# P times V over four heads at once, in place of two heads at a time, in a two-layer attention kernel

## The chip, the cores and the metric

The kernel runs on one core of a Trainium2 chip, with data in float32. The metric is the device time of one execution in microseconds (us), as the median of several runs. The engines are called as the profile calls them: PE is TensorE (PEld its weight loads), DVE VectorE, ACT ScalarE, POOL GpSimd, SP SyncE.

## The reference

Two attention layers, A and B, each on its own input of 2048 rows by 1024, with 32 heads of width 32. A is dilated: each row attends to 8 keys, two rows apart. B is a sliding block, and it is the layer that the change touches:

```python
def _B_ref(x, wqkv, wo):
    B, S, D = x.shape
    H = 32; Dh = D // H; W = 256
    qkv = (x @ wqkv).reshape(B, S, 3, H, Dh).transpose(2, 0, 3, 1, 4)
    q, k, v = qkv[0], qkv[1], qkv[2]
    scores = jnp.einsum("bhqd,bhkd->bhqk", q, k) * (Dh ** -0.5)
    idx = jnp.arange(S)
    mask = (idx[:, None] - idx[None, :] >= 0) & (idx[:, None] - idx[None, :] < W)
    scores = jnp.where(mask[None, None], scores, -1e9)
    p = _softmax(scores, axis=-1)
    o = jnp.einsum("bhqk,bhkd->bhqd", p, v)
    return o.transpose(0, 2, 1, 3).reshape(B, S, D) @ wo
```

The outputs of A and B are concatenated.

## The kernel before

**Units and head groups.** The work is cut into eight units: four chunks of 512 rows of layer B, then four of layer A. Within a unit, the 32 heads are taken in eight groups of four heads. For a unit the kernel computes the projections to Q and K (L579) and to V (L644), the attention of each head group, and, staggered into the next unit, the output projection (L707). These large products run as three float32r matmuls each, on a high and a low part of each operand; VectorE and ScalarE make these parts from raw loads (L213, L216, L219).

**Attention of one head group in layer B.** `attention(u, s)` has two stages. In the first, 16 score matmuls (L959), a masked maximum (L964) and an exponential with a sum (L969) give the logarithm of each row's softmax sum, which is written into extra rows of the stacked Q (L998, L1004). In the second, the scores are computed anew, transposed, keys on partitions (L1043), the exponential is written as P to `pbuf` (L1050), and the triangles at the diagonal and at the far end are cleared by POOL (L1028) or DVE (L1031). Last, `values(li)` multiplies P by V (L1109). The second stage goes in two lots, `li` 0 and 1, each with its scores, exponentials, masks and one run of L1109.

**P times V.** The 128 keys of a block are cut in two halves of 64 (`r` 0 and 1), because the band of a half reaches over fewer query columns (64 + 256 at most). A matmul takes 64 keys (64 rows of the PE array, partitions 64r to 64r+63), 32 columns of V (head `j`, columns 32j to 32j+31 of the array), and streams up to 384 query columns of P. So there are eight tiles of the array, one for each pair of half and head. The half `r` = 0 accumulates in the PSUM tile `o`, the half `r` = 1 in the PSUM tile `x`, head j in partitions 32j to 32j+31 of both; `join` adds the two (L910, L915). `pieces[li]` lists the pieces of columns as (n, r, kb, q0, c): n columns of half r of key block kb. In the first unit there are no earlier keys (`has_halo` is false) and a lot has four pieces: 320, 384, 256 and 192 columns in lot 0, 320, 320, 128 and 64 in lot 1. In units 1 to 3 a lot has six: in lot 0 o 320, x 320, o 256, x 192, x 128, o 64. Each float32 matmul of the program stands in the trace as two passes, each with its own weight load.

**What sets the order.** A planner in Python (`Clock`, and the loop at the end) writes the order of the whole program out: it keeps an estimate of each engine's time and at each step takes, from the queues of attention steps (`ones`, `twos`, `aux`) and projection steps (`gemm`), the one that is ready first. A step of L1109 is one item, with a cost that the change leaves as it is. On each engine the instructions then stand in that order, and semaphores make them wait for each other. The masks of one lot are all planned to be over before its L1109 begins (`values_ready`).

**Copies of Q and K.** SP issues the copies that stack Q and K (L540) and the halo of keys (L469, L530). `later` in `evac` holds a copy back until the head group before last is through with the buffer.

Of the kernel before, what the change touches and what calls it, by code (L numbers as in the profile page):

```python
# [240 lines left out]
def kernel(ctx, tc, xs, wqk, wv, wo, outs, units):  # L241


    nc = tc.nc
# [21 lines left out]
    def parts_of(u):  # L266
        return VPARTS if len(V_AT[u]) == 3 else VPARTS_LATER
# [40 lines left out]
    for p in plan:  # L308
# [3 lines left out]
        elif p[0] == "v":  # L312
            if slots_of(p[1]).get(NG - 1) == p[2] and p[1] + 1 < U:
                continue
            s0, n = parts_of(p[1])[p[2]]
# [10 lines left out]
        else:  # L326
            u = p[1] - 1
# [8 lines left out]
    for key, i in where.items():  # L336
        u = min(key[1] + (key[0] == "o"), U - 1)
        light[i] = PACE[u][5] if units[u][2] else PACE[u][2]
    pbuf = const.tile([P, 4, NP], F32, name="pbuf")
# [73 lines left out]
    done, waiting = {}, {}  # L413
# [4 lines left out]
    class Ring:  # L418
# [21 lines left out]
        def join(self, pool, tag, t):  # L440
            i = len(self.slots)
            self.slots = self.slots[self.i:] + self.slots[:self.i] + [(pool, tag, i)]
            self.i, self.free[i] = 0, t
# [13 lines left out]
    def qk_items(u, s):  # L457
# [3 lines left out]
        hg = u * NG + s  # L461
# [4 lines left out]
        def read_halo():  # L466
            hb = halo[(u + 1) % 2][s]
            for r, a in enumerate((0, 1, 0)):
                nc.sync.dma_start(kst[buf][r:96:3, :, :256].bitcast(F32), hb[:, a])  # L469
                ck.copy("halo_in", ck.now)  # L470

        def evac_window(t, ps, bank):
            if t == 0:
                h2["qk"] = natp.tile([P, 2 * S + 16], F32R, tag="nat", name="nat").bitcast(F32)[:, :2 * S + 8]
                nc.scalar.activation(h2["qk"][:, :S], ps, AF.Copy, scale=SCALE)
                e = ck.use("act", 0.485, ck.now + ck.SEM)
                by_head(0, S, e)
            else:
                qk = h2["qk"]
                nc.scalar.copy(qk[:, S + 8:], ps)  # L480
                e = ck.use("act", 0.485, ck.now + ck.SEM)
                if has_halo:
                    nc.scalar.copy(qk[:, S:S + 8], tails[:, s, :])
                    e = ck.use("act", 0.2, e)
                else:
                    nc.vector.memset(qk[:, S:S + 8], 0.0)
                    ck.use("dve", 0.08, ck.now)
                if u + 1 < U and units[u + 1][3]:
                    nc.scalar.copy(tails[:, s, :], ps[:, S - 8:])
                    e = ck.use("act", 0.2, e)  # L490
                by_head(S, 2 * S + 8, e)
            rg.give(bank, e)
# [18 lines left out]
        def evac(t, ps, bank):  # L511
            if not dense:
                return evac_window(t, ps, bank)
            hl = natp.tile([P, 2 * S + 16], F32R, tag="nat", name="nat")[:, :2 * S].rearrange("p (a s) -> p a s", a=2)
            sc = SCALE if t == 0 else 1.0
            nc.scalar.activation(hl[:, 0, :], ps, AF.Copy, scale=sc)
            r = ck.use("act", 0.485, ck.now + ck.SEM)

            def low():
                nc.vector.scalar_tensor_tensor(hl[:, 1, :], ps, sc, hl[:, 0, :].bitcast(F32), op0=ALU.mult,  # L520
                                               op1=ALU.subtract)
                e = ck.use("dve", 0.61, r)
                rg.give(bank, e)

                def stack():
                    e2 = place(1, e)
                    if t == 1:
                        done["stack"][u, s] = max(e2, h2["hi"]) + PACE[u][1]
                    if t == 1 and u + 1 < U and units[u + 1][3]:
                        nc.sync.dma_start(halo[u % 2][s], hl[:, :, 256:].bitcast(F32))  # L530
                        e2 = ck.copy("halo_out", e, ck.now)
                    done["nat"][2 * hg + t] = max(e2, h2["hi"])

                later(stack)

            def place(part, e):
                dst, c = (qst[buf], 0) if t == 0 else (kst[buf], 256)
                for i, a in enumerate((0, 0, 1) if t == 0 else (0, 1, 0)):
                    if a == part:
                        nc.sync.dma_start(dst[i:96:3, :, c:c + S].bitcast(F32), hl[:, a, :].bitcast(F32))  # L540
                        e2 = ck.copy("copy", e, ck.now)
                return e2

            def stack_hi():
                if t == 0 and has_halo:
                    read_halo()
                h2["hi"] = place(0, r)

            def later(f):
                if hg < 2 or hg - 2 in done["second"]:  # L550
                    f()
                else:
                    waiting.setdefault(hg - 2, []).append(f)

            later(stack_hi)
            ck.defer(r, low)

        for t in range(2):
            h = {}
# [306 lines left out]
    def seat_free(hg):  # L866

        done["scores"][hg] = ck.now

        def go():  # L870
            for f in waiting.pop(("seat", hg), []):
                f()

        ck.defer(ck.now + 0.3, go)
# [61 lines left out]
    def attention(u, s):  # L936
# [4 lines left out]
        hg = u * NG + s  # L941
        q, kk = qst[buf], kst[buf]
        vp, vc = vparts[parts_of(u)][s]
        v = vbufs[parts_of(u)][vp]
        h = {"left": 16, "rows": None}
# [132 lines left out]
        pieces = []  # L1078
        for lot in lots:
            p = []  # L1080
            for kb, c, w in [x for segs, heads in lot for x in segs if heads[0] == 0]:
                q0 = max(0, kb * P)
# [5 lines left out]
            while rows_of[0] or rows_of[1]:  # L1088
                r = 0 if rows_of[0] and (not rows_of[1] or t[0] <= t[1]) else 1
# [11 lines left out]
        def values(li):  # L1101
            if not li:
                h["o"], h["begun"] = [ro.take()[0], rx.take()[0]], set()
            for j0 in (0, 2):
                for n, r, kb, q0, c in pieces[li][0]:
                    slot = (4 * u + kb) % 6
                    part = slice(64 * r, 64 * r + 64)
                    for j in (j0, j0 + 1):
                        nc.tensor.matmul(h["o"][r][32 * j:32 * j + 32, q0:q0 + n],  # L1109
                                         v[part, slot, vc + 32 * j:vc + 32 * j + 32], pbuf[part, j, c:c + n],  # L1110
                                         start=(j, r) not in h["begun"], stop=True, skip_group_check=True)
                        h["begun"].add((j, r))

            def after():
                pfree[0] = ck.now
                h["pv", li] = ck.now
                if hg == last_dense and li:
                    seat_free(hg)
                if li:
                    join(u, s, h)  # L1120

            return after

        for li, lot in enumerate(lots):
            for ci, (segs, heads) in enumerate(lot):
                two.append(Item(lambda li=li, ci=ci: second_ready(li, ci), lambda li=li, ci=ci: second(li, ci),
                                len(heads) * sum(x[2] / 2400 + 0.016 for x in segs)))
            two.append(Item(lambda li=li: values_ready(li), lambda li=li: values(li),
                            C3 + PACE[u][4] + pieces[li][1] / 592))
# [43 lines left out]
    n = TAIL  # L1173
# [92 lines left out]
```

## Time and profile before

| | |
|---|---|
| median of 3 runs | 1834.28 us (1830.59 to 1834.33) |
| the profiled execution, its own time | 1833.12 us |
| its span, first to last instruction | 1831.4 us |
| PE busy | 1809.4 us (99%) |
| DVE, ACT, POOL busy | 1245.9 us (68%), 1034.4 us (56%), 370.2 us (20%) |
| L1109, o and x, busy summed over both | 109.7 us and 109.0 us, 1408 passes each |
| mean granted TensorE clock | 0.999 |

The page of the profile gives busy time for each engine and for each group of instructions of one line. Matmuls overlap, so busy times of PE's groups add up to more than their share of the span; the time between the start of one stretch of matmuls and the start of the next instruction says more. The timeline view lists instructions by start, with those of one line and tile that follow each other merged into one row with a count.

### The profile page before, as it was taken

The page shows a single profiled execution, that of the slowest core. Times are in us where ns is not written, and L with a number is a line of the kernel's source. Part 1 is how long each engine was busy: PE and PEld are TensorE (multiplying, and loading weights), DVE is VectorE, ACT ScalarE, POOL GpSimd, SP SyncE. Part 2 cuts the span into 40 slices and gives each one's busy share as a digit, 9 for nine tenths or more (in the row PEclk, how much of TensorE's full clock was granted, in tenths as well). Part 3 has the DMA queues.
Part 4 walks back from the last instruction along what each step waited for, and adds up shares of the span by engine and source line. Part 5 has one row for each costly group of instructions (what it writes and reads, how often), then busy time and mean ns, then how long its engine had stood idle before and what let it go on. Part 6 is the DMA issues. An engine that isn't in the chain of part 4 may idle for free.

```text
span 1831.4 us, 37311 instructions
## 1 busy us (share of the span) xinstructions
PE 1809.4 (99%) x14186; PEld 1504.5 (82%) x14186; DVE 1245.9 (68%) x2632; ACT 1034.4 (56%) x2552; POOL 370.2 (20%) x835
## 2 busy tenths in 40 slices
PE   8999999999999999999999999999999999999999
PEld 6788788888887888788888878888888888878887
DVE  6578866667766567666666486886777567866674
ACT  5567676666666665766666544552445255644452
POOL 3212222233321222322222400011001100110000
PEclk9999999999999999999999999999999999999999
DMA  7355654546545546455455253345335443544332
GB/s 231 101 152 146 175 159 139 156 144 165 156 139 156 150 127 188 121 153 148 129 145 170 66 160 118 128 131 156 128 109 162 133 137 105 162 129 137 118 111 81
DMA packets 109140, 257.38 MB, mean 141 GB/s; under 512 B 14497, under 2 KB 29857, under 8 KB 108961
## 3 DMA queue, kind: packets, MB, share of 16 engines
q0 software_dynamic: 41760, 152.06, 27.0%
q1 hardware_dynamic: 56832, 83.00, 16.9%
q10 hardware_dynamic: 10368, 19.93, 3.0%
q8 instruction: 112, 1.84, 0.4%
q14 instruction: 68, 0.55, 0.1%
HBM read 164.63 MB, written 23.07 MB: 102 GB/s over the span
## 4 chain that ended last, share of the span: by engine, by line
PE 87%; DMA 4%; DVE 3%; issue 3%; ACT 2%; SPq 0%; POOL 0%; ACTq 0%; POOLq 0%; DVEq 0%
PE g L579 29%; PE g L707 15%; PE g L644 13%; PE x L579 6%; PE s L1043 6%; PE s L959 5%; PE o L1109 4%; PE x L707 3%; PE x L644 3%; PE o L843 2%; PE x L1109 1%; PE s L777 1%; DMA kst<-nat 1%; DMA raw<-wqk 1%; DVE w L219 1%
## 5 line engine op out<-in xcount | busy, mean ns | idle before, releaser
L579 PE MATMUL g<-x,w 128*128 128x512 f32 x2544 | 632.0, 393 | 1.8 <-ACT x L213 1.3
L579 PEld LDWEIGHTS g<-x,w 128*128 128x128 f32 x2544 | 473.0, 189 | 93.3 <-ACT x L213 1.8
L964 DVE CUSTOM_DVE_ANT_0 s<-s,mask_d 128x384 f32<-128x384 f32 (+2 forms) x512 | 262.1, 556 | 133.8 <-PE s L959 132.0
L219 DVE TENSOR_TENSOR w<-raw,w 128x512 fp32r<-128x512 f32 x516 | 335.9, 693 | 24.8 <-ACT w L213 18.3
L644 PE MATMUL g<-w,x 128*128 128x256 f32 (+1 forms) x1920 | 342.1, 322 | 1.3 <-DVE w L219 1.3
L969 ACT ACTIVATE s<-s,nm 128x384 f32<-128x384 f32 (+2 forms) x512 | 274.4, 537 | 74.8 <-DVE nm L964 74.2
L644 PEld LDWEIGHTS g<-w,x 128*128 128x128 f32 x1920 | 283.9, 190 | 25.7 <-DVE w L219 2.4
L707 PE MATMUL g<-ot,w 128*128 128x512 f32 x1224 | 301.4, 392 | 0.0
L707 PEld LDWEIGHTS g<-ot,w 128*128 128x128 f32 x1224 | 225.7, 188 | 45.3 <-issue 1.2
L1028 POOL TENSOR_SCALAR_AFFINE_SELECT pbuf<-pbuf 128x256 f32<-128x256 f32 (+1 forms) x504 | 189.3, 405 | 255.5 <-ACT pbuf L1050 237.2
L1050 ACT ACTIVATE pbuf<-s 128x512 f32<-128x512 f32 (+1 forms) x368 | 188.4, 601 | 82.0 <-PE s L1043 81.8
L216 DVE CAST w<-raw 128x1024 fp32r<-128x1024 f32 x189 | 133.8, 708 | 84.3 <-PE g L579 25.6
L163 POOL DMA_DIRECT2D raw<-wqk x126 | 69.5, 551 | 556.3 <-DVE w L219 382.7
L959 PE MATMUL s<-kst,qst 96*128 96x384 f32 (+2 forms) x512 | 143.2, 340 | 9.4 <-DMA kst<-nat 6.4
L579 PE MATMUL x<-x,w 128*128 128x512 f32 x528 | 127.2, 393 | 0.0
L1043 PE MATMUL s<-qst,kst 128*128 128x128 f32 (+2 forms) x704 | 125.1, 307 | 1.6 <-ACT qst L1004 1.2
L1043 PEld LDWEIGHTS s<-qst,kst 128*128 128x128 f32 x704 | 107.3, 189 | 17.3 <-ACT s L969 2.4
L825 ACT COPY wide<-wide 32x256 f32<-32x256 f32 x256 | 103.3, 404 | 28.8 <-DVE wide L816 25.3
L959 PEld LDWEIGHTS s<-kst,qst 96*128 96x128 f32 x512 | 92.3, 189 | 32.5 <-issue 6.0
L579 PEld LDWEIGHTS x<-x,w 128*128 128x128 f32 x528 | 97.9, 188 | 21.8 <-issue 1.2
L1109 PE MATMUL o<-pbuf,vbuf 64*32 64x320 f32 (+4 forms) x1408 | 109.7, 351 | 0.0
L1109 PE MATMUL x<-pbuf,vbuf 64*32 64x320 f32 (+5 forms) x1408 | 109.0, 349 | 0.0
(101 smaller groups left out, 1844.2 us busy)
## 6 DMA issues: line engine op xcount, KB each, us to landing
raw<-wqk POOLq DMA_DIRECT2D x126, 512.0 KB, 3.9
raw<-wv POOLq DMA_DIRECT2D x72, 512.0 KB, 4.2
raw<-wo POOLq DMA_DIRECT2D x64, 512.0 KB, 4.1
qst<-nat SPq DMA_DIRECT2D x96, 256.0 KB, 4.0
kst<-nat SPq DMA_DIRECT2D x96, 256.0 KB, 4.9
raw<-xs POOLq DMA_DIRECT2D x28, 512.0 KB, 4.8
outs<-ost ACTq DMA_DIRECT2D x56, 256.0 KB, 2.3
kst<-halo SPq DMA_DIRECT2D x72, 128.0 KB, 2.7
```

The source lines that it names most:

```text
L216: nc.vector.tensor_copy(t[:, 0, :], raw)
L219: nc.vector.tensor_tensor(t[:, 1, c:c + 512], raw[:, c:c + 512], t[:, 0, c:c + 512].bitcast(F32), op=ALU.subtract)
L579: nc.tensor.matmul(h["ps"], h["w"][:, a, k * P:(k + 1) * P], xt[u][k][:, b, :], start=(k == 0 and i == 0), stop=(k == NK - 1 and i == 2))
L644: nc.tensor.matmul(ps, xt[u][kw * g + k][:, a, p0:p0 + P], h["w"][g][:, c, k], start=(first and t == 0 and half == 0), stop=(last and t == 2),
L707: nc.tensor.matmul(h["ps"], w[:, a, c:c + P], ot[u, k][:, b, :], start=(k == 0 and i == 0), stop=(k == NK - 1 and i == 2))
L959: nc.tensor.matmul(ps[:, :n], q[0:96, j, b * P:(b + 1) * P], kk[0:96, j, c0:c1], start=True, stop=True)
L964: nc.vector.tensor_tensor_reduce(ps[:, :n], ps[:, :n], mask[:, cut:full], scale=-1.0, scalar=BIG, op0=ALU.add, op1=ALU.min, accum_out=nm)
L969: nc.scalar.activation(ps[:, :n], ps[:, :n], AF.Exp, bias=nm, scale=-1.0, accum_out=sm)
L1028: nc.gpsimd.affine_select(w, w, pattern=[[0, m], [step, n]], compare_op=ALU.is_ge, fill=0.0, base=base, channel_multiplier=chan)
L1043: nc.tensor.matmul(ps[:, x:x + w], kk[:, j, 256 + kb * P:256 + (kb + 1) * P], q[:, j, q0:q0 + w], start=True, stop=True)
L1050: nc.scalar.activation(w, ps[:, :m * n].rearrange("p (j n) -> p j n", j=m), AF.Exp)
L1109: nc.tensor.matmul(h["o"][r][32 * j:32 * j + 32, q0:q0 + n], v[part, slot, vc + 32 * j:vc + 32 * j + 32], pbuf[part, j, c:c + n], start=(j ...
```

## The change

The loop over pairs of heads in `values` goes: each piece of columns is multiplied for all four heads, then the next piece. The number of matmuls, their shapes and operands are the same, and so is the planner's cost of the step.

In the same change the condition in `later` becomes stricter: a copy is held back also while earlier copies for the same buffer are still waiting in the list, so that they keep their order. In the built program this moves one group of DMAs: once in the first unit, SP issues three copies of Q ahead of three of K, where before two of K came first. Apart from this and L1109, each engine's list of instructions is the same as before.

```diff
             def later(f):
-                if hg < 2 or hg - 2 in done["second"]:
+                if hg < 2 or hg - 2 in done["second"] and hg - 2 not in waiting:
                     f()
                 else:
                     waiting.setdefault(hg - 2, []).append(f)
...
-            for j0 in (0, 2):
-                for n, r, kb, q0, c in pieces[li][0]:
-                    slot = (4 * u + kb) % 6
-                    part = slice(64 * r, 64 * r + 64)
-                    for j in (j0, j0 + 1):
-                        nc.tensor.matmul(h["o"][r][32 * j:32 * j + 32, q0:q0 + n],
-                                         v[part, slot, vc + 32 * j:vc + 32 * j + 32], pbuf[part, j, c:c + n],
-                                         start=(j, r) not in h["begun"], stop=True, skip_group_check=True)
-                        h["begun"].add((j, r))
+            for n, r, kb, q0, c in pieces[li][0]:
+                slot = (4 * u + kb) % 6
+                part = slice(64 * r, 64 * r + 64)
+                for j in range(4):
+                    nc.tensor.matmul(h["o"][r][32 * j:32 * j + 32, q0:q0 + n],
+                                     v[part, slot, vc + 32 * j:vc + 32 * j + 32], pbuf[part, j, c:c + n],
+                                     start=(j, r) not in h["begun"], stop=True, skip_group_check=True)
+                    h["begun"].add((j, r))
```

The line of the matmul is L1109 before and L1108 after.

## The prediction, as it was made

> **What bounds the kernel now.** I read the page first, for the engine that has no idle time, and the chain that ended last.
>
> ```profile
> span 1831.4 us, 37311 instructions
> PE 1809.4 (99%) x14186; PEld 1504.5 (82%) x14186; DVE 1245.9 (68%) x2632; ACT 1034.4 (56%) x2552; POOL 370.2 (20%) x835
> PE 87%; DMA 4%; DVE 3%; issue 3%; ACT 2%; SPq 0%; POOL 0%; ACTq 0%; POOLq 0%; DVEq 0%
> ```
>
> PE is busy 99% of the span and is 87% of the chain. What shortens PE's own work shortens the run, as long as nothing else becomes late. So the question is how long a stretch of L1109 holds PE. I asked the windows view for the stretch that holds the second to fourth unit of layer B, first for L1109 alone, then for all instructions.
>
> ```profile
> 265.00:1050.00 785.00, 90.28 (x2304) 64.06 (x2304) 1.00 0.51 146
> 265.00:1050.00 785.00, 781.09 (x5880) 654.41 (x5879) 506.52 (x1304) 503.48 (x1283) 225.38 (x545) 1.00 0.51 146
> ```
>
> The columns behind the window's length are busy time and count: PE and PEld in the first row, PE, PEld, DVE, ACT and POOL in the second. These three units have 48 lots (24 head groups, 2 lots each) of 2304/48 = 48 passes, and a lot keeps PE busy for 90.28/48 = 1.88 us. The first unit, earlier, has 16 lots of four pieces, so 4 pieces x 4 heads x 2 = 32 passes. In the 785 us of the window, PE is idle for 3.9 us, while DVE is busy for 65% and ACT for 64%.
>
> Then the timeline of PE, one lot of each kind. First a lot of 32 passes that waits for nothing:
>
> ```profile
> 198.22 0.46 PE L1109 MATMUL o<-pbuf,vbuf 64*32 64x320 f32 x2
> 198.27 0.46 PE L1109 MATMUL o<-pbuf,vbuf 64*32 64x320 f32 x2
> ...
> 198.78 0.44 PE L1109 MATMUL o<-pbuf,vbuf 64*32 64x256 f32 x4
> ...
> 199.37 0.55 PE L1043 MATMUL s<-qst,kst 128*128 128x128 f32 x2
> ```
>
> The second pair of heads starts 0.05 us after the first (198.27 against 198.22), long before the first pair's 256-column passes (198.78), which stand ahead of it in the program. So matmuls of different tiles overtake each other, and all eight tiles work side by side: the lot holds PE for 199.37 - 198.22 = 1.15 us. Now a lot of 48 passes:
>
> ```profile
> 343.70 0.46 PE L1109 MATMUL o<-pbuf,vbuf 64*32 64x320 f32 x2
> 343.71 0.46 PE L1109 MATMUL x<-pbuf,vbuf 64*32 64x320 f32 x2
> 343.99 0.43 PE L1109 MATMUL o<-pbuf,vbuf 64*32 64x320 f32 x2
> 344.00 0.44 PE L1109 MATMUL x<-pbuf,vbuf 64*32 64x320 f32 x2
> 344.26 0.38 PE L1109 MATMUL o<-pbuf,vbuf 64*32 64x256 f32 x2
> 344.27 0.33 PE L1109 MATMUL x<-pbuf,vbuf 64*32 64x192 f32 x2
> 344.30 0.46 PE L1109 MATMUL o<-pbuf,vbuf 64*32 64x320 f32 x2
> ...
> 344.69 0.22 PE L1109 MATMUL o<-pbuf,vbuf 64*32 64x64 f32 x2
> ...
> 344.75 0.50 PE L1109 MATMUL o<-pbuf,vbuf 64*32 64x64 f32 x4
> ...
> 345.35 0.22 PE L1109 MATMUL o<-pbuf,vbuf 64*32 64x64 f32 x2
> 345.52 0.55 PE L1043 MATMUL s<-qst,kst 128*128 128x128 f32 x2
> ```
>
> Here the second pair starts at 344.30, 0.60 us after the first, and its last pass at 345.35, again 0.60 after the first pair's last (344.75). For 0.60 us half of the tiles stand still at the front, and the other half at the back. The count of rows says why. A pair has 24 passes here; when the second pair gets in, 12 of the first have started (six rows of two) and 12 wait. In the lot of 32 a pair has 16 passes, and with four of them started the same 12 wait: there the second pair gets in at once. PE, then, seems to look past about a dozen waiting passes and no further. The lot takes 345.52 - 343.70 = 1.82 us.
>
> **The change, part by part.** The passes, their sizes and tiles stay. What moves is the place of heads 2 and 3 in the list. For each piece the list now has eight passes, a first and a second one for each head. The second pass of a tile waits for its first, so behind the 320 columns of `o` four passes wait, and behind those of `x` four more: eight, under the dozen that PE looked past. So all eight tiles should start together in the long lots too.
>
> *Long lots.* If the other tiles follow after 0.05 us, as at 198.27, a lot is shorter by 0.60 - 0.05 = 0.55 us: 1.27 us. A second way gives the same: the lot at 198.22 has 576 columns for a tile and takes 1.15; this one has 640, and 64 columns take 344.75 - 344.69 = 0.06 a pass, 0.12 for two, which makes 1.27. All 48 are like this one: its busy stretch, to 345.35 + 0.22, is 1.87 us, and the mean was 1.88. 48 x 0.55 = 26.4 us less. The bounds: the start at no delay gives 48 x 0.60 = 28.8. The other way, PE may not be fed fast enough. The nearest row is a stretch of 64 short passes of layer A:
>
> ```profile
> 1107.88 0.93 PE L777 MATMUL s<-pbuf 32*64 32x72 f32 x64
> 1108.74 0.50 PE L644 MATMUL x<-w,x 128*128 128x256 f32 x2
> ```
>
> 64 passes in 0.86 us are 13.4 ns for one. The eighth tile's first pass is the fifteenth in the new list: 14 x 13.4 = 0.19 us late, and the gain is 0.41 x 48 = 19.7 us. I take 0.55, since the rows at 198.22 and 198.27 are of these very tiles.
>
> [...]
>
> *Waits in front of the passes.* The four heads' waits for their masks now stand in the first four matmuls, ahead of every `x` tile. Where a matmul waits for two semaphores, an instruction of its own goes ahead:
>
> ```profile
> L1109 PEldq EVENT_SEMAPHORE  x43: 51/51/51, 72.9 to 1046.3; - x43
> 75.23 0.55 PE L1109 MATMUL o<-pbuf,vbuf 64*32 64x320 f32 x2
> 75.36 0.46 PE L1109 MATMUL x<-pbuf,vbuf 64*32 64x320 f32 x2
> ```
>
> The two rows are of a lot of the first unit that has two of them, for heads 2 and 3; what follows starts in steps of 0.13 us. In the built program 14 matmuls of the 48 long lots have such a double wait (9 before, most of them covered by the 0.60). 14 x 0.13 = 1.8 us at the most, nothing at the least; those of a lot's first head pass while PE still works on the matmuls before it, so I take half, +0.9.
>
> *The 16 short lots.* Heads 2 and 3 can start 0.04 earlier at best (16 x 0.04 = -0.6 us), and the `x` tiles 0.13 later (+2.1). Both pairs already run together there: 0.
>
> *The copies' order.* Three copies of Q go ahead of three of K, once. The scores need all six, and the last is issued no later. SP's rows bound it: the two copies of K that move back took 1.19 us to issue.
>
> ```profile
> 148.69 1.19 SPq L540 DMA_DIRECT2D kst<-nat  x2
> 149.94 2.28 SPq L540 DMA_DIRECT2D qst<-nat  x3
> ```
>
> 0, from -1.2 to +1.2.
>
> *What is late next.* PE comes 0.55 us earlier to whatever follows a lot. Its waits in the three long units (PE, then PEld, whose waits mostly lie beside running matmuls):
>
> ```profile
> PE s L959 <- DMA kst<-nat: 1.9, 2, 1.3
> PE s L959 <- ACT s L969: 0.5, 2, 0.3
> PEld s L959 <- ACT pbuf L1050: 3.3, 6, 1.7
> PEld s L959 <- ACT s L969: 2.0, 5, 0.7
> ```
>
> The eleven waits of PEld for ACT are where a PSUM bank comes free just in time. If each grew by 0.55 that would be 6.0 us; PE itself lost only 0.5 to the one of these kinds shown, about a quarter of PEld's 2.0, so I take a quarter: +1.5, between 0 and 6.0. The waits for copies of K hang on the evacuation of PE's own products, with no lot in between in the cases that I looked at. Mostly ACT is the one that waits:
>
> ```profile
> 346.17 0.60 ACT L1050 ACTIVATE pbuf<-s 128x512 f32<-128x512 f32 x1 [3.17 <-PE s L1043]
> 339.73 1.74 POOL L1028 TENSOR_SCALAR_AFFINE_SELECT pbuf<-pbuf 128x256 f32<-128x256 f32 x5
> ```
>
> *Sum:* -26.4 + 0.9 + 0 + 0 + 1.5 = -24.0 us. The profiled execution took 1833.12 us, 1.7 around its span; 1809.1. The median of before lies 1.2 over it, so I say 1809.5. By the bounds this case alone reaches from -28.8 - 0.6 - 1.2 = -30.6 to -19.7 + 1.8 + 2.1 + 1.2 + 6.0 = -8.6: about 1803 to 1825.
>
> **The rivals.** *Half is given back.* PE, faster by 3% in these units, runs into its producers more often than the eleven places say: weights that DVE splits, banks that ACT frees. At 65% and 64% DVE and ACT have room, which speaks against; that the list of instructions was laid out for the old pace speaks for. Half of 24 is 12: 1821.5.
>
> *No change.* The tiles of one half of the keys could share their way in, so that four heads of `o` in a row go no faster than two; the lots stay at 1.82, and the time at 1833 to 1834. Against it: at 198.22 eight tiles were at work with no loss. [...]
>
> *Slower, by the masks.* Where a mask of head 2 or 3 ends after the lot has begun, the old order had the first pair's work to do meanwhile; in the new one all eight tiles wait. This is what a late mask looks like, in the first unit:
>
> ```profile
> 221.30 1.89 POOL L1028 TENSOR_SCALAR_AFFINE_SELECT pbuf<-pbuf 128x256 f32<-128x256 f32 x3 [0.56 <-ACT pbuf L1050]
> 222.15 0.46 PE L1109 MATMUL o<-pbuf,vbuf 64*32 64x320 f32 x2
> ```
>
> POOL ends at 223.19, 1.04 us after the lot began. A long lot with such a mask would take 1.04 + 1.27 = 2.31, 0.49 more than now, in place of 0.55 less. It decides from 29 of the 48 on: 29 x 0.49 - 19 x 0.55 = +3.8; all 48 give +23.5, 1858. Against it: at 343.70 POOL was through at 339.73 + 1.74 = 341.47, 2.2 us ahead, and I found none of the 48 with a mask that ends after its start.
>
> **How the numbers follow.** A measurement of this kernel tells about 0.2%, 3.7 us, from no change. The forecast gets 0.80 (with the part of its tail below 1804 or above 1821), half given back 0.12, no change 0.04, slower 0.04. Both of the first two are faster, the whole of their ranges with them: 0.92 faster, 0.04 same, 0.04 slower. The range 1804 to 1821 leaves out the 0.08 of the last two, half of the second, and the thin ends of the first.
>
> **What would show it.** In the profile after: in a long lot a row of four or more 320-column passes of `o`, and `x` right behind, all within 0.1 us, and the next matmul some 1.27 us after the lot's start; L1109's busy time in the three units (at its new line) near 48 x (1.88 - 0.55) = 64 us in place of 90.28; PE's idle time there little over 3.9 us. If lots are short but PE idles 10 us more, half was given back, and the waits name where. If the first rows of a long lot are spread over 0.2 us or more, PE is fed too slowly. If lots stay at 1.8, the dozen is not what held back the second pair. A gain under 8.6 us, or none, makes the forecast wrong.

## The result, and the profile after

The changed kernel takes 1809.95 us (median of 4 runs, 1807.62 to 1814.86) against 1832.43 (4 runs, 1829.76 to 1834.33): 22.5 us less, ratio 0.988 with a 95% interval of 0.985 to 0.991. The forecast was 1809.5. In two later sittings the same kernel gave 1809.72 against 1834.84 and 1811.03 against 1834.45.

The profiled execution of the changed kernel is the slowest of its four, 1814.86 us. From its page:

```profile
span 1813.2 us, 37321 instructions
PE 1787.2 (99%) x14186; PEld 1483.7 (82%) x14186; DVE 1246.0 (69%) x2632; ACT 1034.2 (57%) x2552; POOL 367.7 (20%) x835
```

PE still bounds the kernel. Its busy time fell from 1809.4 to 1787.2, that of the other engines hardly moved. The windows view for the line of P times V (L1108 now), in the stretch with the first unit and in the one with the other three:

```profile
60.00:265.00 205.00, 18.69 (x512) 9.29 (x512) 0.98 0.52 145
265.00:1050.00 785.00, 63.00 (x2304) 42.30 (x2304) 1.00 0.52 151
```

The 48 long lots keep PE busy for 63.00 us in place of 90.28, so 0.57 us less for each. And a long lot, in the timeline of PE:

```profile
346.05 0.47 PE L1108 MATMUL o<-pbuf,vbuf 64*32 64x320 f32 x4
346.07 0.47 PE L1108 MATMUL x<-pbuf,vbuf 64*32 64x320 f32 x4
346.34 0.45 PE L1108 MATMUL o<-pbuf,vbuf 64*32 64x320 f32 x4
...
347.10 0.24 PE L1108 MATMUL o<-pbuf,vbuf 64*32 64x64 f32 x4
347.29 0.55 PE L1043 MATMUL s<-qst,kst 128*128 128x128 f32 x2
```

This is the picture that the forecast asked for: four first passes of `o` and, 0.02 us behind, four of `x`, so all eight tiles at work at once. The lot holds PE from 346.05 to 347.29, 1.24 us, where it was 1.82. From its start to the start of what follows, each of the 48 long lots takes between 1.24 and 1.25 us in the trace.

### The profile page after: what moved, and what is told of

It reads as the page before. It is cut to its first block, busy times and chain, and to the rows that moved or that the text cites. A ratio compares the mean times of both kernels' runs of the same rounds, so it can differ in the third digit from the quotient of the medians.

```text
span 1813.2 us, 37321 instructions
## 1 busy us (share of the span) xinstructions
PE 1787.2 (99%) x14186; PEld 1483.7 (82%) x14186; DVE 1246.0 (69%) x2632; ACT 1034.2 (57%) x2552; POOL 367.7 (20%) x835
## 4 chain that ended last, share of the span: by engine, by line
PE 89%; DMA 4%; DVE 3%; ACT 2%; issue 1%; SPq 0%; ACTq 0%; POOL 0%; DVEq 0%; POOLq 0%
PE g L579 30%; PE g L707 15%; PE g L644 13%; PE x L579 6%; PE s L1043 6%; PE s L959 5%; PE o L1108 3%; PE x L707 3%; PE x L644 3%; DMA kst<-nat 2%; PE o L843 2%; PE s L777 1%; PE x L1108 1%; DMA raw<-xs 1%; DVE w L219 1%
## 5 line engine op out<-in xcount | busy, mean ns | idle before, releaser
L644 PE MATMUL g<-w,x 128*128 128x256 f32 (+1 forms) x1920 | 346.8, 325 | 1.1 <-DVE w L219 1.0
L644 PEld LDWEIGHTS g<-w,x 128*128 128x128 f32 x1920 | 288.2, 193 | 26.2 <-DVE w L219 2.6
L969 ACT ACTIVATION_READ_ACCUMULATOR s<-s,nm 128x1 f32 x512 | 105.7, 206 | 0.1
L163 POOL DMA_DIRECT2D raw<-wv x72 | 45.7, 635 | 273.5 <-DVE w L219 191.2
```

The lines of the kernel that those rows point to most:

```text
L163: (self.nc.scalar if early else self.nc.gpsimd).dma_start(raw if len(ap.shape) == 2 else raw.rearrange("p (a b) -> p a b", a=2), ap)
L644: nc.tensor.matmul(ps, xt[u][kw * g + k][:, a, p0:p0 + P], h["w"][g][:, c, k], start=(first and t == 0 and half == 0), stop=(last and t == 2),
L969: nc.scalar.activation(ps[:, :n], ps[:, :n], AF.Exp, bias=nm, scale=-1.0, accum_out=sm)
```

## The experiments

All were timed against the kernel before; the ratio's 95% interval stands in brackets.

### Which half of the change: the copies' order, and the heads' order

The first kernel has only the new condition in `later`, the second only the new loop:

```diff
-                if hg < 2 or hg - 2 in done["second"]:
+                if hg < 2 or hg - 2 in done["second"] and hg - 2 not in waiting:
```

> Only the stricter condition of the copies; heads two at a time as before. Window theory (PE looks past about a dozen waiting passes, so in a long lot the second pair of heads gets in only when 12 of the first pair's 24 passes have started): long lots stay at 1.81 us, the whole at the time before, within 3.7 us. Rival (part of the 22 us comes from the copies): 5 us or more faster with long lots unchanged.

Measured: 1834.54 us against 1833.82, ratio 1.0008 (0.9995 to 1.002). Long lots as before: the windows row for L1109 reads

```profile
265.00:1050.00 785.00, 90.29 (x2304) 64.17 (x2304) 1.00 0.52 146
```

> Only the order of the heads, four at a time; the copies' condition as before. Window theory: long lots 1.24 us, the whole 20 to 26 us faster than before, like the full change within 4 us. Rival (the copies have a part): less than that by 5 us or more.

Measured: 1814.45 against 1833.82, ratio 0.9892 (0.9873 to 0.9911), with the long lots at 63.00 us. That is 19.4 us faster, just under the 20 expected, and its time is 4.5 us above that of the full change in the first sitting, where 4 were expected at most. So both were run again, side by side on one chip:

> The kernel with only the order of the heads once more, beside the full change on the same chip: it was 19.4 us faster than before, the full change 22.5 and 25.1 in other sittings. If the copies' order has no part, the two agree here within 2 us. Rival: with four heads at once the copies' order is worth 3 to 5 us, and this one stays that much behind.

> The full change, beside the kernel with only the order of the heads: within 2 us of it if the copies' order has no part, 3 to 5 us ahead if it has one; 20 to 26 us faster than before.

Measured: 1810.79 for the heads alone, ratio 0.9861 (0.9842 to 0.988), and 1811.03 for the full change, ratio 0.9865 (0.9848 to 0.9881), against 1834.45. They agree within 0.3 us. The copies' order has no part in the gain that these runs can tell (their intervals reach 3.0 to 3.5 us to either side); the order of the heads is all of it.

### How far PE looks past waiting passes

The prediction held that PE looks past about a dozen waiting passes. Two kernels keep two heads at a time, but cut the six pieces of a long lot, so that the first pair stands with fewer passes ahead of the second. These two kernels and the next two have the copies in the new order:

```diff
-            for j0 in (0, 2):
-                for n, r, kb, q0, c in pieces[li][0]:
+            for j0, ps in [(j, pieces[li][0][i:i + 4]) for i in (0, 4) for j in (0, 2)]:
+                for n, r, kb, q0, c in ps:
```

> Still two heads at a time, but of the six pieces of a long lot the first four for heads 0 and 1, the same four for heads 2 and 3, then the last two for each pair. A pair then stands with 16 passes ahead of the other, as in the short lots, which are unchanged. Window theory: 12 wait when four have started, so the second pair starts 0.05 us after the first, long lots take 1.24 to 1.35 us, and the whole is 48 x 0.46 to 0.57 = 22 to 27 us faster than before. Rival (it counts that four heads of one half of the keys stand in a row, so that the halves alternate less often): two heads in a row as before, long lots 1.81 us, no gain.

Measured: 1820.18 us against 1833.82, ratio 0.9925 (0.9904 to 0.9947), 13.6 us faster. The timeline of a long lot:

```profile
345.37 0.46 PE L1109 MATMUL o<-pbuf,vbuf 64*32 64x320 f32 x2
345.38 0.46 PE L1109 MATMUL x<-pbuf,vbuf 64*32 64x320 f32 x2
345.42 0.46 PE L1109 MATMUL o<-pbuf,vbuf 64*32 64x320 f32 x2
...
346.69 0.27 PE L1109 MATMUL x<-pbuf,vbuf 64*32 64x128 f32 x1
346.89 1.13 PE L1043 MATMUL s<-qst,kst 128*128 128x128 f32 x6
```

The second pair starts 0.05 us after the first (345.42), as expected, with two heads in a row as before: that four heads of one half stand in a row is not what gains. But the lot takes 1.52 us (1.43 for lot 1), not 1.24 to 1.35. Its last pieces come late, the last pass at 346.69, 1.32 after the start, and the gain is 13.6 us where 22 to 27 were expected. More on this below.

The kernel with five pieces first (`:i + 5`, `in (0, 5)`):

> As the kernel with four pieces first, but five: a pair stands with 20 passes ahead of the other. Window theory: the second pair gets in when 8 have started, which in the rows of before is 0.30 us after the lot's start, half of 0.60; long lots take 1.50 to 1.58 us, the whole is 48 x 0.23 to 0.31 = 11 to 15 us faster than before. Rival (four in a row): 1.81 us, no gain. A rival in which any cut of the lot is enough: the same as with four pieces first.

Measured: 1833.84 against 1833.82, ratio 1.0002 (0.9992 to 1.0012). No gain, and the timeline says that the dozen is wrong:

```profile
343.44 0.46 PE L1109 MATMUL o<-pbuf,vbuf 64*32 64x320 f32 x2
343.45 0.46 PE L1109 MATMUL x<-pbuf,vbuf 64*32 64x320 f32 x2
343.73 0.43 PE L1109 MATMUL o<-pbuf,vbuf 64*32 64x320 f32 x2
343.75 0.43 PE L1109 MATMUL x<-pbuf,vbuf 64*32 64x320 f32 x2
344.00 0.38 PE L1109 MATMUL o<-pbuf,vbuf 64*32 64x256 f32 x2
344.01 0.33 PE L1109 MATMUL x<-pbuf,vbuf 64*32 64x192 f32 x2
344.03 0.46 PE L1109 MATMUL o<-pbuf,vbuf 64*32 64x320 f32 x2
```

At 343.75 eight of the first pair's 20 passes have started and 12 wait; still the second pair comes only at 344.03, 0.59 after the first, when 8 wait. What is the same in both kernels is the count for one tile. In the kernel before, each tile has six passes of a pair's list. Here, in lot 0, the tiles of `x` have six still (320, 192 and 128 columns, two passes each), and those of `o` four; in the kernel with four pieces first, and in the short lots, all have four, and there nothing waits. In each case the second pair gets in as soon as the tiles with six passes have begun their third (344.01 here, 344.27 in the kernel before). So in these lists the second pair started once no tile had more than four of the first pair's passes left, the running one among them: 0.05 us after the first pair with four passes a tile, 0.59 and 0.60 us after it with six. The dozen was four tiles times three. That the count for one tile decides is the author's reading of these lists: the traces show when passes start, not what holds them back. Each pass comes with its own weight load (1408 of both for `o`, and as many for `x`, in the profile of before), so these runs can't tell whether it is the matmuls or the loads that wait.

This reading and the dozen part widely for one head at a time:

```diff
-            for j0 in (0, 2):
+            for j0 in range(4):
...
-                    for j in (j0, j0 + 1):
+                    for j in (j0,):
```

> One head at a time: all pieces of head 0, then of head 1, and so on; the copies in the new order. A new theory after the kernel with five pieces first: each tile has a queue of its own that takes three waiting passes behind the running one, and the first pass that finds its tile's queue full holds up all behind it. In a long lot a tile has six passes, so each head holds up the next for two passes of 320 columns, 0.58 to 0.60 us: long lots take 1.24 + 3 x 0.59 = 3.0 us, short lots (four passes a tile, all fit) 0.9 to 1.2 as before; the whole is 48 x 1.2 = 57 us slower than before. The old count of a dozen waiting passes in all: long lots 2.1 to 2.2 us, 15 to 20 us slower.

Measured: 1889.06 us against 1834.84, ratio 1.0298 (1.028 to 1.0315): 54.2 us slower, with 57 expected from four passes a tile and 15 to 20 from the dozen. The timeline of a long lot:

```profile
356.14 0.45 PE L1109 MATMUL o<-pbuf,vbuf 64*32 64x320 f32 x1
...
356.71 0.32 PE L1109 MATMUL x<-pbuf,vbuf 64*32 64x192 f32 x1
356.73 0.45 PE L1109 MATMUL o<-pbuf,vbuf 64*32 64x320 f32 x1
...
357.31 0.45 PE L1109 MATMUL o<-pbuf,vbuf 64*32 64x320 f32 x1
...
357.89 0.45 PE L1109 MATMUL o<-pbuf,vbuf 64*32 64x320 f32 x1
...
359.09 1.12 PE L1043 MATMUL s<-qst,kst 128*128 128x128 f32 x6
```

Each head begins 0.58 to 0.59 us after the one before (356.14, 356.73, 357.31, 357.89), right after that one's tiles have begun their third pass, though at most ten of its passes wait at a time. The lot takes 2.95 us.

### Why the last pieces came late

With four pieces first for each pair, the last two pieces stood by pairs too. Here they run over all four heads:

```diff
+            for hs, ps in (((0, 1), pieces[li][0][:4]), ((2, 3), pieces[li][0][:4]), (range(4), pieces[li][0][4:])):
+                for n, r, kb, q0, c in ps:
```

> As the kernel with four pieces first for each pair of heads, but the last two pieces run over all four heads. Three waiting passes a tile: the second pair starts 0.05 us after the first as there; whether the last pieces still come late is open. If their order by pairs made them late, long lots fall from 1.52 and 1.43 to 1.24 to 1.30 us and the whole is 20 to 25 us faster than the kernel before. If the late last pieces come from the two pairs' first pieces, lots stay at 1.4 to 1.5 and the gain at 14 us.

Measured: 1819.61 against 1834.84, ratio 0.9921 (0.9902 to 0.9939), 15.2 us faster; long lots 1.45 and 1.43 us. So the order of the last pieces has a part of 0.07 us in lot 0 and none in lot 1; the rest of the delay is not from it. The end of a long lot:

```profile
346.83 0.33 PE L1109 MATMUL x<-pbuf,vbuf 64*32 64x128 f32 x4
346.93 0.22 PE L1109 MATMUL o<-pbuf,vbuf 64*32 64x64 f32 x1
...
347.11 0.34 PE L1109 MATMUL o<-pbuf,vbuf 64*32 64x64 f32 x7
347.38 0.55 PE L1043 MATMUL s<-qst,kst 128*128 128x128 f32 x2
```

One first pass of 64 columns starts at 346.93, 0.10 us after the row of 128 columns (346.83), and the other seven start from 347.11 on, 0.28 us after it. In the changed kernel, with the same last pieces in the same order, the two rows of 64 columns start at 347.04 and 347.10, 0.08 and 0.14 us after the first row of 128 columns (346.96). Four passes a tile does not explain this stall of 0.18 us, and no run here settles what does: it stays open. It concerns these two trial orders alone, not the change.

### The changed kernel again, and its clock

> The changed kernel once more, for its size and its clock. Long lots 1.24 us; 20 to 25 us faster than before. If the lower granted clock of its first runs (0.995 to 0.997, where runs of before had 0.995 to 1.000, mostly 0.997 to 0.999) goes with the change, the mean here is again 0.001 to 0.002 lower than that of the runs of before; if it was chance, the means agree within 0.0005.

Measured: 1809.72 against 1834.84, ratio 0.9867 (0.9853 to 0.988). That is 25.1 us faster. The granted clock (the share of its full speed that PE's clock was given) of its runs was 0.9970 in the mean, that of the runs of before 0.9972: here they agree. But in the third sitting the changed kernel had 0.9960 and the kernel before 0.9971, while the kernel with the heads' order alone had 0.9972. By the measure that was set, the clock is lower in one of these two sittings and not in the other; whether a lower clock goes with the change stays open. It is worth little: 0.001 x 1810 = 1.8 us, as an estimate.

### A plan laid out for the new pace

```diff
-                                C3 + PACE[u][4] + pieces[li][1] / 592))
+                                0.15 + pieces[li][1] / 592))
```

> The changed kernel with the planner's cost for a lot set to the measured hold, 0.15 us and 1/592 us for a column (1.23 for a long lot, 1.12 and 0.91 for the short ones); the whole order is laid out anew. Theory that the list laid out for the old pace loses little: within 4 us of the changed kernel. Rival (half of the loss of 4 to 5 us against the sum of the lots comes from the old layout): 2 to 6 us faster than the changed kernel.

Measured: 1825.64 against 1834.84, ratio 0.9955 (0.9941 to 0.9969): 16 us slower than the changed kernel in the same sitting. Neither theory said that. Its page, and two rows of its waits (PEld's and PE's: us in total, times, longest):

```profile
span 1823.0 us, 37318 instructions
PE 1790.0 (98%) x14186; PEld 1484.7 (81%) x14186; DVE 1251.8 (69%) x2646; ACT 1030.8 (57%) x2549; POOL 367.2 (20%) x824
```

```profile
PEld o L1108 <- POOL pbuf L1028: 3.9, 7, 1.5
```

```profile
PE o L843 <- ACT wide L828: 4.0, 2, 2.9
```

PE is idle for 1823.0 - 1790.0 = 33.0 us, where the profile of the changed kernel in the same sitting has 1807.7 - 1783.4 = 24.3. Little of this is waiting for masks in front of a lot: 3.9 us in 7 waits of PEld, against 2.2 in 4. The rest is spread over other waits, such as the second row's, in layer A, and one of 2.30 us in which the output projection behind a long lot waits for that lot's own sum. The granted clock was lower too, 0.994 in the mean against 0.997; 0.003 x 1823 = 5.5 us is an estimate of what that costs. The planner's cost for a lot was too high by up to a quarter of a microsecond, and set right it brought waits. Whether the margin itself or the other order that came out of it did the harm was not tried apart.

## Why the prediction was right, and where it was not

- **Long lots, -26.4 us.** Measured 90.28 - 63.00 = 27.3. The delay of the second pair of heads went from 0.60 us to a few hundredths, as taken, and a lot takes 1.24 us, where 1.27 was forecast.
- **The reason for the delay.** Here a step failed: "PE, then, seems to look past about a dozen waiting passes and no further". In the kernel with five pieces first the second pair stayed out with 12 passes waiting and came 0.59 us late, with 8; in the one with one head at a time each head came 0.58 to 0.59 us late, though at most ten waited. In both the start fell at the third pass of the tiles that had six. Both counts allow the new order, which gives all tiles their passes evenly, and `x` did start 0.02 us behind `o`, so the forecast stood. That the wrong count did no harm to it was luck: that waiting passes of the first pair go with a late second pair held in every list with six passes to a tile, the limit did not. A forecast for 20 passes made from the dozen was wrong by all of its 11 to 15 us.
- **The order of starts.** In the profile of before, the 320-column passes of heads 2 and 3 at 198.27 start ahead of 256-column passes, at 198.78, that stand before them in the program. And the order in the program bears on the time: kernels with the same passes in different orders took from 1810 to 1889 us.
- **Waits in front of the passes, +0.9.** Not to be seen: the long lots with double waits take 1.24 us like the rest.
- **Short lots, 0.** Mis-sized: 20.21 - 18.69 = 1.5 us less, outside the bounds of -0.6 to +2.1. In the trace most of those lots took 0.93 to 1.23 us before and take 0.89 or 1.13 now; the steps of 0.13 at double waits are gone. Why they no longer cost was not tested.
- **The copies' order, 0.** No effect seen in the kernels with each half, as finely as they tell: the copies alone gave -0.9 to +3.7 us.
- **What is late next, +1.5.** In the long units PE's idle time went from 3.9 us to 4.7 us:

```profile
269.80:1030.86 761.06, 756.37 (x5880) 633.99 (x5879) 506.89 (x1304) 503.17 (x1283) 224.99 (x545) 1.00 0.52 150
```

```profile
PE s L959 <- DMA kst<-nat: 3.3, 3, 2.1
PEld s L959 <- ACT pbuf L1050: 2.7, 5, 1.0
PEld s L959 <- ACT s L969: 2.2, 8, 0.6
```

The first is the windows view of the same instructions, now 761 us long (PE, PEld, DVE, ACT, POOL); the others are waits in it. PEld's waits for ACT, 3.3 and 2.0 us before, have not grown together, and the 1.5 us priced on them did not come. What grew in this profile is PE's wait for copies of K, 1.9 us before, which the prediction had put at nothing; two later profiles of the same kernel have 2.9 and 1.7, so not much can be made of it. Little was given back here. Over the whole span PE's idle time went from 22.0 to 26.0 us in this profile.

- **The sum.** -24.0 forecast, of which the lots and their waits made -26.4 + 0.9 = -25.5; they gave -27.3 - 1.5 = -28.8. The profiled pair differ by 18.3 us only. Idle time takes 4.0 of the difference of 10.5. The rest, 6.5 us, fits a lower granted clock, 0.995 in the mean against 0.999: the last section has three stretches of half clock that the profile of before lacks, 3.4 + 6.8 + 3.4 = 13.6 us at a clock of 0.50; half of their length, 6.8 us, is an estimate of what they cost. The profile of the changed kernel in the second sitting, at a clock of 0.998, spans 1807.7 us, 23.7 less than the 1831.4 of before. The medians, -22.5, -25.1 and -23.4 in three sittings, lie around the forecast. That it was met so closely is in part luck: the lots brought 3.3 us more than forecast, and about as much more than forecast was given back, to idle time and the clock as far as the profiles tell. (The prediction's own steps, 1809.1 and 1.2 more, make 1810.3; it wrote 1809.5.)
- **The rivals.** Half given back: no, the waits above did not grow so. No change: no, the long lots take 1.24 us. Slower by the masks: no; the two lots of the first unit with late masks took 2.20 and 1.56 us before and take 2.21 and 1.57 now. The plan with the lower cost has more such waits, at a small size.

## What to carry to other kernels

Where small matmuls share the array as tiles, try an order that deals passes to all tiles in turn: here the same 48 passes took 1.24 us so, and 1.82 or 2.95 us in lists that gave a tile six passes before the next heads had any. That is not all: pairs of heads with four passes a tile each took 1.43 to 1.52 us, by a stall that was not explained. What the order costs does not show as idle time of PE, which was 99% busy before and after; it shows when the starts of passes in one stretch are compared with a stretch of the same kind that is not held up. And a plan laid out with a cost that is too high is not mended by the cost alone: with the measured one, the new plan took 16 us more.

## What the runs showed of the hardware that was not expected

The windows view for 180 to 200 us of both kernels, before first and then after, has the granted clock behind POOL's count:

```profile
180.00:200.00 20.00, 16.85 (x152) 15.68 (x151) 19.40 (x56) 13.07 (x39) 5.14 (x11) 1.00 0.66 193
```

```profile
180.00:200.00 20.00, 17.00 (x135) 15.85 (x134) 17.47 (x50) 12.30 (x36) 3.85 (x8) 0.83 0.68 189
```

In both, PE waits some 3 us for a copy of K in this stretch, 3.14 us before and 3.00 after. The timeline of the changed kernel has the wait in its last column:

```profile
188.12 1.09 PE L959 MATMUL s<-kst,qst 96*128 96x128 f32 x4 [3.00 <-DMA kst<-nat]
```

In the changed kernel the clock then was 0.83 over the 20 us, which is worth 20 x 0.17 = 3.4 us, as an estimate; in the profile of before it was 1.00, after the same wait. The profile of the changed kernel has two more such stretches that the profile of before lacks, each behind a shorter wait of PE, one of 1.33 us that ends at 49.95 and one of 2.09 us that ends at 712.69. The windows view of the three, first to last, has a clock of 0.50 in each; the second begins while the wait of 3.00 us still lasts:

```profile
50.50:53.90 3.40, 3.40 (x8) 2.67 (x9) 1.62 (x7) 2.56 (x9) 1.06 (x3) 0.50 0.11 16
187.10:193.90 6.80, 5.78 (x27) 5.77 (x28) 5.52 (x19) 2.11 (x10) 1.06 (x2) 0.50 0.63 221
712.70:716.10 3.40, 3.40 (x15) 3.40 (x16) 3.40 (x11) 0.00 (x0) 0.72 (x1) 0.50 0.22 59
```

So waits of 1.33, 2.09 and 3.00 us came with a clock of 0.50 here, and the longer wait of 3.14 us in the profile of before came with 1.00: the length of the wait alone does not tell, and what does is not shown. In the two other profiles of the changed kernel the stretch of 180 to 200 us had 0.83 again, and the kernel with only the new copies' order, as slow as before, had 0.91 there; so it does not need the new order of the heads. Whether the new order makes it longer is not shown. This scatter of a few microseconds is a part of why the profiled pair differ by less than the medians.
